# A tap-weighted sum with a routed expert layer: scheduler margins in two phases, constants in a chain of their own, tap weights of two units in the logits' place

## The chip, the cores and the metric

The kernel runs on one core of a Trainium2 chip, whose engines each take their instructions in order and meet through semaphores: PE (matrix products), VectorE (DVE in the profile), ScalarE (ACT), GpSimd (POOL) and SyncE (SP), which issues most of the DMA transfers. The metric is the device time of one execution in microseconds. Before the change three runs took 1194.86, 1198.12 and 1200.12 us, median 1198.12.

## The reference

The input x is 8 sequences of 3584 rows of 192 numbers, in 8 heads of 24. Each row and head has 7 tap weights; their softmax weighs the row and the six before it. The result, 28672 rows, goes through a routed layer of 8 experts, one for each row.

```python
w = softmax(weight_gen, axis=-1)                     # (8, 3584, 8 heads, 7 taps)
x = einsum('bshk,bskhg->bshg', w, windows of 7 rows of x, zeros in front)   # -> (28672, 192)
logits = x @ w_gate                                  # 8 experts
e_idx  = argmax(logits, axis=1)
gate_w = softmax(logits)[row, e_idx]
eom    = sigmoid(x @ w_output_gate)[row, e_idx]
for e in range(8):                                   # rows of expert e only
    out[rows] = gate_w * eom * (relu(x[rows] @ w1[e]) @ w2[e])    # 192 -> 1024 -> 192
```

## The kernel before

The rows are cut into 32 units of 896 (128 partitions by 7 rows). A unit goes through these steps. Its tap weights are loaded (w) and made into a softmax on VectorE and ScalarE. Its seven products of taps and rows are shared: GpSimd makes the first ones (gap), VectorE the others (vap, or vt from unit 7 on). TAPS says how many; 4 of 7 go to GpSimd in units 0 to 6, and 4 to 6 later, by POOL and SHARES. In units 0 to 6 (PE_U) PE adds the seven products up in PSUM with an identity matrix (constants cf); from unit 7 on VectorE adds them. ScalarE and VectorE then split the sum into a high and a low half of 16 bits in a record (rt, three buffers in turn), beginning with the row numbers (rt from tok). That first write needs the scatters of the unit three before, which read the same buffer, to have landed. The record is transposed (gt), by PE and a copy of ScalarE in units below TR_U, by seven DMA transposes on SP's queue in the others. Three matmuls a row group give the logits (gm, gt). VectorE finds the expert (lz to the scan p), PE the ranks (p with upper and ones), and after that the rows' places are known (pos, posi). GpSimd then issues seven indirect transfers that scatter the unit's records into the expert-sorted array srtd in DRAM. p_4 means the scan of unit 4, and so on.

Beside this the weights of the 8 experts are loaded, scaled, split into halves and stored in DRAM (wd). The low halves wa and wpb are VectorE instructions with two inputs in SBUF.

As soon as all weights are there and the first three units have been sorted, tiles of 256, later 384 and 512 rows of one expert are taken from srtd: 77 tiles in all, 229 groups of 128 rows. SP loads a tile's row numbers (meta), its transposed rows (xT) and the expert's two weight arrays (wa, wb). GEMM1 (xT, wa) fills a PSUM bank; ScalarE makes the high half of its relu (hh) and VectorE the low half (hl); GEMM2 (wb with hh and hl) gives the output, which ScalarE scales (ys). The first tiles' output (DEFER of them) goes to DRAM by SP (yd) and is scattered at the end; that of later tiles is scattered by GpSimd at once. Units and tiles run beside each other until the last unit is sorted, near 913 us; then only tiles are left.

The order of every engine's instructions is written when the program is built. Each step above is a chain, a generator that names the engine of its next instruction. A planner keeps a clock and times for each engine; at each step it takes the chain that could go on first by its own estimates, that is by `max(now, c.t - c.slack, c.engine.t - c.engine.lead) - c.favour`, and by rank where these are equal. The numbers behind it are margins: LAT and its kin are added after an instruction until its result counts as there, LEAD is how far SP may be filled ahead, WBX delays the return of a weight buffer, FAVOUR is a table by chain number. They act through the order alone. On the chip every engine goes through its list, and an instruction waits for what it reads.

The PSUM has fixed places: two sums of units (0 and 2560), the tap weights of units below 7 (3904 and 1344), the logits (2048), the turned records (1536), small tables. At the end of the front they become banks of GEMM1 and GEMM2.

Of the kernel before, what the change touches and what calls it, by code (L numbers as in the profile page):

```python
# [67 lines left out]
class Chain:  # L68


    def __init__(self, gen, rank, t, engine):
        self.gen, self.rank, self.t, self.engine, self.gate = gen, rank, t, engine, None
        self.favour = 0.0
        self.slack = EAGER[1] if len(rank) > 1 and rank[0] in EAGER[2] and rank[1] < EAGER[0] else SLACK


class Order:
# [5 lines left out]

    def add(self, gen, rank, engine, t=None):
        c = Chain(gen, rank, self.cur.t if t is None else t, engine)
        c.favour = FAVOUR.get(self.made, 0.0)
# [24 lines left out]
class Queue:  # L111


    def __init__(self, order, engine, cost, issue, lead, host=None):
        self.order, self.engine, self.cost, self.issue, self.lead, self.host = order, engine, cost, issue, 0.0 if host else lead, host
        self.moved = self.issued = 0.0

# [24 lines left out]
class Paced:  # L142


    def __init__(self, order, engine, cost, before=0.0, after=None, lead=0.0, follows=True, holds=None):
        self.order, self.engine, self.cost, self.t = order, engine, cost, 0.0
        self.before, self.after = before, LAT if after is None else after
        self.lead, self.follows, self.holds = lead, follows, holds

    def __getattr__(self, name):  # L150
        f = getattr(self.engine, name)

        def call(*args, **kwargs):
            c, own = self.order.cur, self.cost(name, args, kwargs)
            r = f(*args, **kwargs)  # L155
            if own is not None:
                held = LOCK and self.holds is not None and self.holds(kwargs)
                self.t = max(self.t, (c.t if self.follows else self.order.now) + self.before, self.order.port if held else 0.0) + own
                if held:
                    self.order.port = self.t  # L160
                c.t = max(c.t, self.t + self.after)
            return r

        return call


def two_in_sbuf(kwargs):
    return sum(k in kwargs and kwargs[k].space != bass.MemoryType.PSUM for k in ("in0", "in1", "data0", "data1")) > 1
# [23 lines left out]
def gpsimd_cost(name, args, kwargs):  # L192
    if name == "indirect_dma_start":
        return 0.987
    if name == "memset":
        return 1.0
    return 0.172 + largest(args, kwargs) * 0.002
# [23 lines left out]
def kernel(ctx: ExitStack, tc: tile.TileContext, x, wg, wgate, wogate, w1, w2, cst, out):  # L221
    nc = tc.nc
    od = Order()
    V = Paced(od, nc.vector, vector_cost, holds=two_in_sbuf)
    S = Paced(od, nc.scalar, scalar_cost, after=LAT_S)
    G = Paced(od, nc.gpsimd, gpsimd_cost, holds=lambda kwargs: True)
    T_ = Paced(od, nc.tensor, tensor_cost, after=0.0)
    SP = Queue(od, nc.sync, sync_cost, sync_issue, LEAD)
    TQ = SP if TURN_SP else Queue(od, nc.scalar, sync_cost, sync_issue, LEAD, S)
# [139 lines left out]
    nc.vector.tensor_copy(f_e8, cf[:, o : o + 8])  # L369
# [11 lines left out]
    nc.vector.tensor_copy(f_rr, rr[:, :, 0])  # L381
# [27 lines left out]


# [44 lines left out]
    def weight_steps(stg):  # L455

        for e in range(NE):
            yield from take(st_free, SP)

            st1 = stg.tile([P, 1536], F32, tag="st1", name=f"st1_{e}")  # L460
            st2 = stg.tile([P, 1536], F32, tag="st2", name=f"st2_{e}")
            SP.dma_start(out=st1[:, 0:1024], in_=w1[e, 0:128, :])
            for h in range(2):
                SP.dma_start(out=st1[64 * h : 64 * h + 64, 1024:1536], in_=w1[e, 128:192, 512 * h : 512 * h + 512])
            SP.dma_start(out=st2.rearrange("p (c d) -> p c d", d=D), in_=w2[e].rearrange("(c p) d -> p c d", p=P))
            od.add(split_steps(e, st1, st2), (RANK_W, e), S)
# [3 lines left out]
            od.cur.t = od.now  # L470

    def split_steps(e, st1, st2):
# [18 lines left out]
        for lo, n in ((0, 1024), (2048, 512)):  # L491
            src = st1[:, lo // 2 : lo // 2 + n]
            hi = wah[:, lo : lo + n]
            yield S
            S.activation(hi, src, AF.Copy, scale=s1)
            yield V
            V.scalar_tensor_tensor(out=wah[:, lo + n : lo + 2 * n], in0=src, scalar=s1, in1=hi, op0=ALU.mult, op1=ALU.subtract)
# [15 lines left out]
        S.activation(hi, st2, AF.Copy, scale=s2)  # L513
        yield V
        V.scalar_tensor_tensor(out=wbh[:, 1536:3072], in0=st2, scalar=s2, in1=hi, op0=ALU.mult, op1=ALU.subtract)
# [102 lines left out]
    def acc_steps(u, taps):  # L618
# [8 lines left out]
        while own or left:  # L627
            yield V, lambda: own or gp
            if own and not (n and gp and gp[0][2] <= od.now + SLACK):
# [27 lines left out]
    def used(u, tag):  # L657
# [3 lines left out]
        if tag == "va":  # L661
            (tw_free if u >= PE_U - 2 and d["tw_at"] == 3904 else d["tw_home"]).append((od.cur.t, d["tw_at"]))
# [5 lines left out]
    def add_steps(u, t, tag, kind):  # L668
# [12 lines left out]
        tap_free[tag].append((od.cur.t + LAT_P, kind))  # L681
        if n == K - 1 - PAIRS:
            d["total"] = d["sum"][:, 0 : NV * GD].rearrange("p (a b) -> p a b", b=GD)
            od.add(sum_steps(u), (RANK_B, u), S, T_.t + LAT_P)

    def sum_steps(u):
# [39 lines left out]
        else:  # L726
            od.cur.t += LAT_T
# [36 lines left out]
        od.cur.t += LAT_R  # L764
# [261 lines left out]
    def gemm1_unit(hp, d, u, at):  # L1026
# [10 lines left out]
        od.add(evac_steps(d, ps[:, at : at + nf * T], hh[:, 0 : nf * T], hl[:, 0 : nf * T], at, u), (RANK_H,), S, T_.t + LAT_P)  # L1037
# [10 lines left out]
    def gemm2_group(d, g, at):  # L1048
# [126 lines left out]
    od.add(softmax_steps(0), (RANK_A, 0, 0), V, U[0]["wt"])  # L1175
    od.add(gate_steps(), (RANK_GATE, -1), SP)
# [68 lines left out]
def TAPS(u):  # L1245

    n = PRO_G if u < PE_U else FIRST_G[u - PE_U] if u < PE_U + len(FIRST_G) else SHARES.get(u, POOL[u % len(POOL)])
# [7 lines left out]
LAT = 0.226  # L1255
LAT_S = 0.191
LAT_P = 0.485
LAT_T = 3.005
LOCK = False
LAT_R = 1.0  # L1260
SLACK = 0.026
EAGER = 0, 0.2, (2, 3, 4)
LEAD = 3.739
# [4 lines left out]
AHEAD = 1  # L1268
DELAY = {128: 4, 256: 1, 384: 1, 512: 1}
LATE = 4  # L1270
# [5 lines left out]
PRO_G = 4  # L1276
POOL = (5,5,4)
SHARES = {7: 5, 8: 6, 15: 4, 22: 5, 29: 4, 30: 5}
FAVOUR = {32: 2.7, 117: 2.9, 447: 0.5, 448: 0.4, 553: 1.5, 689: 3.2, 706: 1.8, 874: -0.2, 886: 2.1, 925: 4.0, 941: -0.4, 1008: -1.4}
PE_U = 7  # L1280
GIVE = 1
RANK_X = 2.5
X_EARLY = 3
RANK_GATE = 3.985
FIRST_G = ()
DEFER = 4
WBX = 5.532
# [3 lines left out]
TR_U = 5  # L1291
# [21 lines left out]
```

## Time and profile before

| | before |
|---|---|
| runs, us | 1194.86, 1198.12, 1200.12 (median 1198.12) |
| profiled execution, us | 1196.09 (span 1194.3) |
| PE busy | 1114.0 us, 93% of the span |
| VectorE busy | 944.6 us, 79% |
| ScalarE busy | 594.9 us, 50% |
| GpSimd busy | 857.5 us, 72% |
| granted clock of PE, mean | 0.979 |

The shares are means over a front, where only units are worked on, a middle, where units and tiles run together, and a tail with tiles alone. The busy tenths by slice of a fortieth of the span (29.9 us) show them: PE stands at 6 to 8 in the first eight slices and at 9 after; VectorE at 6 to 8 in the first seven, 9 in the middle and 1 to 3 in the tail. PEclk is the granted clock of PE in tenths of full speed.

### The profile page before, as it was taken

To read this page: it belongs to the slowest core of one execution; us is meant where nothing else is said; L and a number is where in the kernel's file an instruction comes from. 1 tells how busy PE (TensorE), PEld (TensorE's weight loads), DVE (VectorE), ACT (ScalarE), POOL (GpSimd) and SP (SyncE) were. 2 spreads that over 40 slices of the span, in tenths; PEclk is the share of its full clock that TensorE was granted. 3 is DMA by queue.
4 is the path that set the end of the run, shared out by engine and by line. 5 is a ranking of instruction groups with operands and counts; after the bars stand their busy time and mean duration, and the time that the engine had idled before them with its cause. 6 is when DMAs were issued, how large, how long until landed. Compare 5 with 4: busy or idle time off the path is not lost.

```text
span 1194.3 us, 27270 instructions
## 1 busy us (share of the span) xinstructions
PE 1114.0 (93%) x9689; PEld 812.9 (68%) x9689; DVE 944.6 (79%) x2009; ACT 594.9 (50%) x1257; POOL 857.5 (72%) x758
## 2 busy tenths in 40 slices
PE   6978776699999999999999999999999999999897
PEld 2444345577766767777777777777777777899697
DVE  6788966889999999999999999998999763333231
ACT  2857534455555555555555555555555543434342
POOL 5685779777888888888888888888888752422222
PEclk9988898899999999999999999999999999999999
DMA  9896768999998788898688996986877579889992
GB/s 286 262 300 197 235 185 209 261 296 251 247 269 228 226 249 239 238 262 236 190 247 246 252 247 195 270 238 188 256 211 220 163 212 328 254 265 349 328 307 84
DMA packets 274937, 290.40 MB, mean 243 GB/s; under 512 B 213238, under 2 KB 238311, under 8 KB 265072
## 3 DMA queue, kind: packets, MB, share of 16 engines
q1 hardware_dynamic: 252912, 244.06, 70.8%
q0 software_dynamic: 21744, 44.30, 11.8%
q8 instruction: 76, 1.25, 0.4%
q14 instruction: 61, 0.50, 0.1%
q10 hardware_dynamic: 144, 0.29, 0.1%
HBM read 186.54 MB, written 61.42 MB: 208 GB/s over the span
## 4 chain that ended last, share of the span: by engine, by line
PE 65%; DVE 13%; DMA 7%; issue 5%; POOL 4%; SPq 4%; ACT 1%; POOLq 0%; DVEq 0%; ACTq 0%
PE ps L155 65%; DVE ps L155 5%; SPq L129 4%; DVE hl L155 3%; DMA wa<-wd 3%; POOL gap L155 2%; POOL srtd L155 2%; DMA srtd<-rt,posi 1%; DVE vt L155 1%; DMA wd<-wa 1%; DVE rt L155 1%; POOL out_dram L155 1%; DVE wa L155 1%; DVE vap L155 1%; DVE wpb L155 1%
## 5 line engine op out<-in xcount | busy, mean ns | idle before, releaser
L155 PE MATMUL ps<-xT,wa 128*128 128x512 f16 (+3 forms) x2480 | 488.1, 346 | 34.6 <-DVE hl L155 15.8
L155 PE MATMUL ps<-wb,hh 128*128 128x192 f16 x3664 | 472.9, 246 | 0.2 <-DVE hl L155 0.2
L155 PE MATMUL ps<-wb,hl 128*128 128x192 f16 x1832 | 451.1, 246 | 0.0
L155 DVE SCALAR_TENSOR_TENSOR hl<-ps,hh 128x512 f16<-128x512 f32 (+1 forms) x472 | 308.0, 665 | 153.4 <-ACT hh L155 149.4
L155 ACT ACTIVATE hh<-ps 128x512 f16<-128x512 f32 (+1 forms) x472 | 272.8, 583 | 230.7 <-PE ps L155 224.3
L155 PEld LDWEIGHTS <-wa 128*128 128x128 f16 x2480 | 226.7, 98 | 212.6 <-issue 21.3
L155 PEld LDWEIGHTS <-hh 128*128 128x128 f16 x3664 | 333.4, 98 | 43.1 <-issue 1.3
L155 POOL TENSOR_TENSOR gap<-x,w 128x768 f32<-128x768 f32 (+5 forms) x254 | 343.3, 1376 | 23.6 <-PE ps L155 14.2
L155 POOL DMA_INDIRECT out_dram<-ys,meta x221 | 219.4, 993 | 189.7 <-ACT ys L155 143.9
L155 POOL DMA_INDIRECT srtd<-rt,posi x224 | 226.5, 1011 | 85.4 <-issue 56.8
L155 ACT ACTIVATE ys<-ps,sc 128x192 f32<-128x192 f32 x229 | 96.2, 420 | 221.9 <-PE ps L155 157.2
L155 DVE TENSOR_TENSOR ps<-ps,gap 128x1344 f32<-128x1344 f32 x118 | 182.9, 1550 | 3.7 <-POOL gap L155 3.2
L155 PEld LDWEIGHTS <-hl 128*128 128x128 f16 x1832 | 179.6, 98 | 0.1
L155 PE MATMUL ps<-vap,cf 128*128 128x512 f32 (+1 forms) x126 | 60.6, 626 | 16.0 <-DVE vap L155 16.0
L155 POOL TENSOR_TENSOR gap<-halo,w 128x1152 f32<-128x1152 f32 (+5 forms) x38 | 60.0, 1580 | 18.9 <-ACT gt L155 10.8
L155 PE MATMUL ps<-gap,cf 128*128 128x512 f32 x168 | 69.7, 551 | 0.0
L155 DVE SCALAR_TENSOR_TENSOR rt<-ps,sx,rt 128x448 f16<-128x448 f32 x64 | 58.0, 909 | 7.7 <-ACT rt L155 3.8
L155 PE MATMUL ps<-xT,late 128*128 128x128 f16 (+2 forms) x560 | 55.4, 256 | 4.0 <-DMA late<-wd 4.0
L155 PEld LDWEIGHTS ps<-vap,cf 128*128 128x128 f32 x126 | 25.9, 217 | 43.2 <-issue 23.6
L155 PEld LDWEIGHTS ps<-gap,cf 128*128 128x128 f32 x168 | 30.4, 192 | 29.4 <-issue 24.8
L155 DVE TENSOR_TENSOR ps<-ps,vt 128x1344 f32<-128x1344 f32 x32 | 49.7, 1552 | 0.0
L155 DVE TENSOR_TENSOR vt<-x,ps 128x1344 f32<-128x1344 f32 (+2 forms) x39 | 49.6, 1284 | 0.1
(122 smaller groups left out, 813.2 us busy)
## 6 DMA issues: line engine op xcount, KB each, us to landing
wa<-wd SPq DMA_DIRECT2D x62, 1024.0 KB
wb<-wd SPq DMA_DIRECT2D x76, 768.5 KB
x<-in_x_dram SPq DMA_DIRECT2D x32, 672.0 KB
late<-wd SPq DMA_DIRECT2D x14, 1024.0 KB
w<-in_wg_dram SPq DMA_DIRECT2D x32, 196.0 KB
wd<-wpb SPq DMA_DIRECT2D x8, 768.5 KB
st<-in_w_dram SPq DMA_DIRECT2D x8, 768.0 KB
st<-in_w_dram SPq DMA_DIRECT2D x8, 512.0 KB
```

The source lines that it names most:

```text
L129: r = f(*args, **kwargs)
L155: r = f(*args, **kwargs)
```

## The change

The numbers of the planner become two sets, FIRST until its clock is at 395 us and LATER from then on, and many get other values. With LOCK the planner now counts VectorE instructions with two inputs in SBUF and GpSimd's products as excluding each other. A negative favour delays a chain. The constants f_e8 and f_rr are copied in a chain of their own. VectorE's tap weights of units 1 and 2 stand in the logits' place. Units 5 and 6 are turned by PE (TR_U 7). GpSimd's taps fall in units 8 (6 to 4), 12, 27 and 30 (5 to 4) and rise in unit 15 (4 to 5). FRONT, WEIGHT_RANKS and LOW_G change nothing by themselves, since their values are those that held before or are empty.

```diff
 class Order:
+    def m(self, name):
+        return (FIRST if self.now < TURN else LATER)[name]
 ...
-            at = max(self.now, c.t - c.slack, c.engine.t - c.engine.lead)
-            key = (at - c.favour, c.rank)
+            at = max(self.now, c.t - c.slack - min(0.0, c.favour), c.engine.t - c.engine.lead)
+            key = (at - max(0.0, c.favour), c.rank)
 ...
-    nc.vector.tensor_copy(f_e8, cf[:, o : o + 8])
+    e8 = cf[:, o : o + 8]
 ...
-    nc.vector.tensor_copy(f_rr, rr[:, :, 0])
 ...
+    def const_steps():
+        V.tensor_copy(f_e8, e8)
+        V.tensor_copy(f_rr, rr[:, :, 0])
 ...
-        home = tw_free if u >= PE_U else rest_free
+        home = tw_free if u >= PE_U else lg_free if u in TW_LG else rest_free
 ...
+        if u == PE_U - 1:
+            tw_free.extend(f for f in rest_free if f[1] == 3904)
+            rest_free[:] = [f for f in rest_free if f[1] != 3904]
 ...
-        t, _ = sum_free.pop()
-        acc_free.append(t)
+        got = next(f for f in sum_free if f[1] == 2560)
+        sum_free.remove(got)
+        acc_free.append(got[0])
 ...
+    od.add(const_steps(), (RANK_A, 0, 1), V, CONST_AT)
 ...
-LAT = 0.226
 ...
-LEAD = 3.739
+FIRST = {'LAT': 0.083, 'LAT_S': 0.191, 'LAT_P': 0.295, 'LAT_T': 1.952, 'LAT_R': 1.0, 'LOCK': True, 'SLACK': 0.02, 'LEAD': 5.44, 'G_D': 0.987, 'WBX': 3.688}
 ...
+CONST_AT = 10.0
+TW_LG = (1, 2)
-AHEAD = 1
+AHEAD = 2
-LATE = 4
+LATE = 2
-SHARES = {7: 5, 8: 6, 15: 4, 22: 5, 29: 4, 30: 5}
+SHARES = {12: 4, 27: 4, 30: 4}
-GIVE = 1
+GIVE = 2
-DEFER = 4
+DEFER = 6
-TR_U = 5
+TR_U = 7
```

What this does to the order is shown at three places. In the names the first number is that of the unit or tile: gap6_2 is the product of unit 6 and tap 2, p3_4 the scan of unit 4, xT0 the first tile, rt_2_101 the third record buffer (units 2, 5, 8), rt_0_99 the first (units 0, 3, 6).

PE, at the first GEMM1. Before, it stands behind the ranks of unit 4 and one product of unit 6:

```order
L155 MATMUL ps_82<-gap6_1_1305,cf_91 128x512 x2
L155 MATMUL ps_82<-gap6_1_1305,cf_91 128x320
L155 LDWEIGHTS upper_94
L155 MATMUL ps_82<-p3_4_1369,upper_94 128x8
L155 LDWEIGHTS ones16_97
L155 MATMUL ps_82<-p3_4_1369,ones16_97 128x8
L155 MATMUL ps_82<-gap6_2_1364,cf_91 128x512 x2
L155 MATMUL ps_82<-gap6_2_1364,cf_91 128x320
L155 LDWEIGHTS wa2_138
L155 MATMUL ps_82<-xT0_1389,wa2_138 128x256
```

After, it stands behind the last logits of unit 5 and that unit's ranks:

```order
L161 LDWEIGHTS gt5_1420
L161 MATMUL ps_82<-gm_251,gt5_1420 128x32
L161 LDWEIGHTS gt5_1420
L161 MATMUL ps_82<-gm_251,gt5_1420 128x32
L161 LDWEIGHTS upper_94
L161 MATMUL ps_82<-p3_5_1601,upper_94 128x8
L161 LDWEIGHTS ones16_97
L161 MATMUL ps_82<-p3_5_1601,ones16_97 128x8
L161 LDWEIGHTS wa2_136
L161 MATMUL ps_82<-xT0_1306,wa2_136 128x256
```

All 49 products of units 0 to 6 and the turning of unit 5 have moved ahead of it; that of unit 6 now stands between the blocks of the first tile's GEMM1.

SP, between the second and the third tile's loads. Before, the seven transposes of unit 5 stand there (those of unit 6 follow the third tile, those of unit 7 the fifth):

```order
L129 DMA wb1_1485<-wd_79 128x1537
L129 DMA_TRANSPOSE gt5_1518<-rt_2_101 128x3x128 x7
L129 TENSOR_LOAD ti2_0_1058
L129 ISA x2
L1014 ISA
L129 DMA meta2_1603<-srtd_78 128x2x2
L129 ISA
L129 DMA_TRANSPOSE xT2_1605<-srtd_78 128x3x256
L129 ISA
L129 DMA wa1_137<-wd_79 128x2048
L129 ISA
L129 DMA wb2_1608<-wd_79 128x1537
```

After, the third tile (meta2, xT2, wa1, wb2) follows directly on the second, and the loads of units 8 and 9 behind it:

```order
L136 DMA wb1_1364<-wd_79 128x1537
L136 TENSOR_LOAD ti2_0_1056
L136 ISA x2
L1036 ISA
L136 DMA meta2_1436<-srtd_78 128x2x2
L136 ISA
L136 DMA_TRANSPOSE xT2_1438<-srtd_78 128x3x256
L136 ISA
L136 DMA wa1_135<-wd_79 128x2048
L136 ISA
L136 DMA wb2_1441<-wd_79 128x1537
L136 DMA halo_83<-in_x_dram 112x1152
```

The first DMA transposes are now those of unit 7, and stand behind the sixth tile's load.

ScalarE, at the record of unit 6, which waits for the landing of unit 3. Before, it stands between two high halves (hh0) of the first tile:

```order
L155 ACTIVATE rt_1_100<-ez4_1424,isx4_1134 128x7
L155 ACTIVATE hh0_0_1444<-ps_82 128x512
L155 ACTIVATE hh0_1_1529<-ps_82 128x512
L155 ACTIVATE rt_0_99<-tok_102 128x7x2
L155 ACTIVATE rt_0_99,ssq6_1561<-ps_82 128x7x192
L155 ACTIVATE hh0_2_1549<-ps_82 128x512
L155 ACTIVATE rt_0_99<-ps_82,sx6_1568 128x7x192
L155 ACTIVATE hh0_3_1579<-ps_82 128x512
```

After, it stands ahead of the last copy of unit 5's turned rows, and all high halves follow later:

```order
L161 COPY gt5_1420<-ps_82 128x768
L161 CAST posi4_1506<-pos4_1503 128x7
L161 ACTIVATE rt_1_100<-ez4_1465,isx4_1151 128x7
L161 COPY gt5_1420<-ps_82 128x768
L161 ACTIVATE w8_1285<-w8_1285 128x392
L161 ACTIVATE rt_0_99<-tok_102 128x7x2
L161 ACTIVATE rt_0_99,ssq6_1565<-ps_82 128x7x192
L161 COPY gt5_1420<-ps_82 128x384
L161 ACTIVATE rt_0_99<-ps_82,sx6_1577 128x7x192
```

On GpSimd the scatters of units 3 and 4 alternated; after, all seven of unit 3 are issued ahead of unit 4's.

## Rows read from the trace of the kernel before

**Rows 1.** Windows of the whole run: us, each engine's busy time (instructions), PEclk, DMA share, GB/s.

```profile
0.00:163.00 163.00, 129.00 (x510) 66.44 (x511) 130.29 (x274) 91.66 (x151) 109.86 (x90) 0.94 0.79 246
163.00:193.00 30.00, 16.36 (x85) 10.11 (x84) 12.98 (x43) 10.28 (x20) 25.51 (x23) 0.83 0.84 221
193.00:305.00 112.00, 98.40 (x982) 80.94 (x979) 102.17 (x235) 55.97 (x137) 86.55 (x75) 0.95 0.93 260
305.00:500.00 195.00, 189.82 (x1661) 136.98 (x1662) 187.83 (x400) 103.03 (x228) 166.23 (x148) 0.99 0.86 245
500.00:913.00 413.00, 411.55 (x3631) 295.74 (x3629) 397.14 (x819) 220.32 (x479) 361.64 (x320) 1.00 0.82 230
913.00:1195.00 282.00, 268.88 (x2829) 222.67 (x2826) 114.19 (x243) 113.65 (x245) 107.71 (x107) 0.99 0.81 254
```

**Rows 2.** Waits of PE, whole run: us in total, times, longest us.

```profile
PE ps L155 <- DVE hl L155: 16.0, 12, 10.3
...
PE ps L155 <- DMA wa<-wd: 11.9, 7, 5.0
```

**Rows 3.** Timeline of PE: start, duration, instructions [idle before <- releaser].

```profile
187.86 2.29 PE L155 MATMUL ps<-xT,wa 128*128 128x256 f16 x10 [10.31 <-DVE hl L155]
...
192.90 0.33 PE L155 MATMUL ps<-wb,hh 128*128 128x192 f16 x2
...
214.66 1.67 PE L155 MATMUL ps<-xT,wa 128*128 128x256 f16 x7 [6.56 <-DVE ez L155]
...
238.61 1.49 PE L155 MATMUL ps<-xT,wa 128*128 128x384 f16 x5 [4.96 <-DMA wa<-wd]
```

**Rows 4.** Timeline of ACT.

```profile
150.37 0.80 ACT L155 COPY gt<-ps 128x768 f16<-128x768 f16 x1 [2.58 <-PE ps L155]
...
184.97 0.22 ACT L155 ACTIVATE rt<-tok 128x14 int32<-128x14 f32 x1 [9.44 <-DMA srtd<-rt,posi]
```

**Rows 5.** Timeline of SP's queue.

```profile
176.33 10.48 SPq L129 DMA_TRANSPOSE gt<-rt  x7
...
217.60 9.81 SPq L129 DMA_TRANSPOSE gt<-rt  x7
...
231.24 0.42 SPq L129 DMA_DIRECT2D wa<-wd  x1
```

**Rows 6.** Timeline of DVE at the start.

```profile
4.45 0.17 DVE L369 COPY ps<-cf 128x8 f32<-128x8 f32 x1 [4.45 <-DMA cf<-in_cst_dram]
...
6.00 0.57 DVE L155 TENSOR_REDUCE ps<-w 128x56 f32<-128x392 f32 x1
```

**Rows 7.** Timeline of DVE, units 3, 4 and 5.

```profile
157.00 0.20 DVE L155 TENSOR_REDUCE pos<-pe 128x7 f32<-128x56 f32 x1
...
163.14 0.26 DVE L155 TENSOR_TENSOR_SCAN p<-segs,ps 128x56 f16<-128x56 f16 x1
...
205.49 0.26 DVE L155 TENSOR_TENSOR_SCAN p<-segs,ps 128x56 f16<-128x56 f16 x1
```

**Rows 8.** Timeline of POOL.

```profile
99.70 2.22 POOL L155 TENSOR_TENSOR gap<-halo,w 128x1152 f32<-128x1152 f32 x1 [10.75 <-ACT gt L155]
...
158.87 0.98 POOL L155 DMA_INDIRECT srtd<-rt,posi  x1 [2.25 <-ACT rt L155]
...
163.78 2.72 POOL L155 TENSOR_TENSOR gap<-x,w 128x576 f32<-128x576 f32 x2
...
178.12 0.98 POOL L155 DMA_INDIRECT srtd<-rt,posi  x1 [0.30 <-issue]
```

**Rows 9.** Groups of PE by form, 0 to 170 us: busy us, mean ns.

```profile
L155 PE MATMUL ps<-ident,rt 128*128 128x128 f16 x105 | 10.2, 236 | 1.4 <-DVE ps L155 1.4
```

**Rows 10.** Groups of DVE by form, whole run.

```profile
L155 DVE TENSOR_TENSOR vt<-x,ps 128x1344 f32<-128x1344 f32 x24 | 37.0, 1541 | 0.0
```

**Rows 11.** Timeline of DVE, low halves of two experts' weights.

```profile
106.91 3.46 DVE L155 SCALAR_TENSOR_TENSOR wa<-st,wsc,wa 128x512 f16<-128x512 f32 x1
...
125.42 0.69 DVE L155 SCALAR_TENSOR_TENSOR wa<-st,wsc,wa 128x512 f16<-128x512 f32 x1
```

More of the change, by code (lines that the diff above doesn't have):

```diff
@@ L73, in __init__ @@
         self.favour = 0.0
-        self.slack = EAGER[1] if len(rank) > 1 and rank[0] in EAGER[2] and rank[1] < EAGER[0] else SLACK
+        self.slack = 0.0
 class Order:
@@ L111, with __init__, lead @@
 class Queue:
-    def __init__(self, order, engine, cost, issue, lead, host=None):
-        self.order, self.engine, self.cost, self.issue, self.lead, self.host = order, engine, cost, issue, 0.0 if host else lead, host
+    def __init__(self, order, engine, cost, issue, host=None):
+        self.order, self.engine, self.cost, self.issue, self.host = order, engine, cost, issue, host
         self.moved = self.issued = 0.0
+    @property
+    def lead(self):
+        return 0.0 if self.host is not None else self.order.m("LEAD")
     @property
@@ L142, with __init__ @@
 class Paced:
-    def __init__(self, order, engine, cost, before=0.0, after=None, lead=0.0, follows=True, holds=None):
+    def __init__(self, order, engine, cost, after, holds=None):
         self.order, self.engine, self.cost, self.t = order, engine, cost, 0.0
-        self.before, self.after = before, LAT if after is None else after
-        self.lead, self.follows, self.holds = lead, follows, holds
+        self.after, self.lead, self.holds = after, 0.0, holds
     def __getattr__(self, name):
@@ L156, in call, with two_in_sbuf @@
             if own is not None:
-                held = LOCK and self.holds is not None and self.holds(kwargs)
-                self.t = max(self.t, (c.t if self.follows else self.order.now) + self.before, self.order.port if held else 0.0) + own
+                held = self.order.m("LOCK") and self.holds is not None and self.holds(name, kwargs)
+                self.t = max(self.t, c.t, self.order.port if held else 0.0) + own
                 if held:
                     self.order.port = self.t
-                c.t = max(c.t, self.t + self.after)
+                c.t = max(c.t, self.t + (self.order.m(self.after) if self.after else 0.0))
             return r
         return call
-def two_in_sbuf(kwargs):
-    return sum(k in kwargs and kwargs[k].space != bass.MemoryType.PSUM for k in ("in0", "in1", "data0", "data1")) > 1
+def two_in_sbuf(name, kwargs):
+    return name in ("tensor_tensor", "scalar_tensor_tensor") and sum(k in kwargs and kwargs[k].space != bass.MemoryType.PSUM for k in ("in0", "in1", "data0", "data1")) > 1
 def largest(args, kwargs):
@@ L189, in scalar_cost, with gpsimd_cost @@
     return own + (0.2 if "accum_out" in kwargs else 0.0) + (0.0 if isinstance(kwargs.get("scale", 1.0), float) else 0.1)
[L192 removed]
+def gpsimd_cost(name, args, kwargs, scatter):
     if name == "indirect_dma_start":
[L194 removed]
+        return scatter
     if name == "memset":
         return 1.0
[L197 removed]
+    return 0.13 + largest(args, kwargs) * 0.00184
 def tensor_cost(name, args, kwargs):
@@ L223 @@
     od = Order()
[L224 to L229, printed above, removed]
+    V = Paced(od, nc.vector, vector_cost, "LAT", holds=two_in_sbuf)
+    S = Paced(od, nc.scalar, scalar_cost, "LAT_S")
+    G = Paced(od, nc.gpsimd, lambda *o: gpsimd_cost(*o, od.m("G_D")), "LAT", holds=lambda name, kwargs: name in ("tensor_tensor", "scalar_tensor_tensor"))
+    T_ = Paced(od, nc.tensor, tensor_cost, None)
+    SP = Queue(od, nc.sync, sync_cost, sync_issue)
+    TQ = SP if TURN_SP else Queue(od, nc.scalar, sync_cost, sync_issue, S)
     B, SEQ, D = x.shape
@@ L470, in weight_steps, with halves @@
             od.cur.t = od.now
+    def halves(which, hi, low, src, scale):
+        if which in LOW_G:
+            S.activation(src, src, AF.Copy, scale=scale)
+            S.copy(hi, src)
+            yield G
+            G.tensor_tensor(out=low, in0=src, in1=hi, op=ALU.subtract)
+        else:
+            S.activation(hi, src, AF.Copy, scale=scale)
+            yield V
+            V.scalar_tensor_tensor(out=low, in0=src, scalar=scale, in1=hi, op0=ALU.mult, op1=ALU.subtract)
     def split_steps(e, st1, st2):
@@ L489, in split_steps @@
         wah = wa.bitcast(F16)
-        for lo, n in ((0, 1024), (2048, 512)):
+        for part, (lo, n) in enumerate(((0, 1024), (2048, 512))):
             src = st1[:, lo // 2 : lo // 2 + n]
@@ L494, in split_steps @@
             yield S
-            S.activation(hi, src, AF.Copy, scale=s1)
-            yield V
-            V.scalar_tensor_tensor(out=wah[:, lo + n : lo + 2 * n], in0=src, scalar=s1, in1=hi, op0=ALU.mult, op1=ALU.subtract)
+            yield from halves((e, part), hi, wah[:, lo + n : lo + 2 * n], src, s1)
         yield SP
@@ L512, in split_steps @@
         S.activation(wb.bitcast(F32)[:, 1536:1537], inv[:, 0:1], AF.Copy, scale=inv[:, 1:2])
-        S.activation(hi, st2, AF.Copy, scale=s2)
-        yield V
-        V.scalar_tensor_tensor(out=wbh[:, 1536:3072], in0=st2, scalar=s2, in1=hi, op0=ALU.mult, op1=ALU.subtract)
+        yield from halves((e, 2), hi, wbh[:, 1536:3072], st2, s2)
         st_free.append(od.cur.t)
@@ L628, in acc_steps @@
             yield V, lambda: own or gp
-            if own and not (n and gp and gp[0][2] <= od.now + SLACK):
+            if own and not (n and gp and gp[0][2] <= od.now + od.m("SLACK")):
                 k = own.pop(0)
```

42 lines of the change are left out of this document (21 added, 21 removed).

## The prediction

> **What bounds the kernel now.** I read the windows first, cut where the kernel changes its nature [rows 1]. Until 163 us no engine is the bound: PE and VectorE are each busy about 130 us, so the end of this stretch is set by the chain from unit to unit. From 163 to 193 the first tile starts and everything starves: PE 16.4 of 30 us, VectorE 13.0, granted clock 0.83. From 193 to 305 (the first nine tiles) PE works 98.4 of 112 us. From 305 to 913 it works 601.4 of 608 and VectorE 585.0, so both are nearly full. In the last 282 us PE has 268.9 and VectorE only 114. What can be won lies before 305; what can be lost lies between 305 and 913, where VectorE has 23 us left over.
>
> The waits of PE name the pieces [rows 2], and its timeline gives the dates [rows 3]. At 187.86 PE resumes after 10.31 us without work, and that block of ten matmuls took 2.29 us, which I put down to the lower clock around it. At 214.66 it has waited 6.56 us in the unit chain, at 238.61 4.96 us for a tile's weights. The first GEMM2 is at 192.90. The causes stand on other engines. ScalarE's record write of unit 6 (rt from tok) sat from 175.5 to 184.97 on the landing of unit 3's scatters, and the next hh of the first tile is behind it [rows 4]. SP's queue spent 10.48 us and later 9.81 us on seven transposes each between tile loads; after the second group a tile's weights were asked for only at 231.24, and PE's 4.96 us followed [rows 5].
>
> **The change part by part.** Sums are against the profiled execution, 1196.1 us, 2 us under the median of the runs (1198.1). The work that an order puts before a given instruction I took by giving each instruction its group's mean duration in the trace of before, less the 0.06 us by which neighbours overlap where stretches are compared.
>
> *Constants.* VectorE waited 4.45 us for cf, then did memsets and two copies until 6.00, when the first softmax began without a wait [rows 6]. After, the memsets run while cf and w are on their way, and the copies (0.17 and 0.19 us) come behind two products. The first softmax can start when w is there, somewhere before 6.00. Bounds 0 and -4.4; I take -1.5, the memsets and copies that stood behind cf, and count it in the date of p_5 below.
>
> *Unit chain and the first tile.* Before, GEMM1 began directly behind p_4's ranks; after, behind p_5's, with all 49 taps and five more turn rounds ahead of it. VectorE's work up to the scan of p_5 falls from 171.8 to 153.2 us; up to p_4's, dated 163.14, it was 143.7 [rows 7]. With the same idle time p_5's scan comes at 163.1 + 153.2 - 143.7 = 172.6. But it hangs on the landing too: ScalarE now has unit 6's record write ahead of unit 5's last gt copy. In before unit 3's position came at 157.00 and its first scatter at 158.87; its last was issued at 178.12, since POOL alternated units 3 and 4, and landed 6.85 us later [rows 4, 7, 8]. After, VectorE has 9.8 us less ahead of that position, which gives about 146; seven scatters at 0.98 with a little between them and four products of 2.72 follow in one run [rows 8], so the last is issued near 166 and has landed at 173. Record write, squares, copy and logits take some 4 us, the rank chain 3.5: p_5's scan at 177 to 181 (before: 205.49). VectorE then has 9.3 us ahead of the first tile's first low half, while PE does GEMM1 and turns unit 6. First GEMM2 near 189: -4.
>
> The two added transposed units cost PE 42 transposes at 10.2/105 = 0.097 us [rows 9], 4.1 us, and ScalarE eight copies of at most 0.80 [rows 4]. They lie mostly beside the chain before 189; at worst the full 4.1 adds. TAPS of units 1 and 2 in the logits' place only delay unit 0's logits, at 60 us or so, covered by products; bounds 0 and +6.6, the one wait of PE in the unit chain that the rows price [rows 3]; taken 0.
>
> *First nine tiles.* The three tile loads stand together in SP's queue, and fourteen of its transposes, 20.3 us [rows 5], are gone; so the 6.56 and the 4.96 us should go [rows 3]. The order puts 95.2 us of PE work between the first and the tenth tile (before 96.0) and 93.2 of VectorE's (before 102.8), so PE decides. Before needed 112 with 13.6 of it idle; I expect about 4 idle, -9 to -10, since some waits return: three banks instead of four until unit 6 is turned, and unit 7's seven transposes come just behind tile 6's load. Tenth tile near 291 instead of 305: -14. Bounds -22 (every idle microsecond from 163 to 305 except the chain's) and 0.
>
> *Tiles ten to 45.* SHARES moves four products from GpSimd to VectorE, 4 x 1.54 = 6.2 us [rows 10], and work that the front no longer does comes here as well: VectorE's order holds 604.7 us in this stretch, before 592.0, against 598.5 of PE in both. Before took 608 us. VectorE would fill 99% of that, so some low halves come late; I take +4. Bounds: 0, if the idle share of PE hides it, and +13, if VectorE keeps the ratio of before (592.0/608, so 604.7 takes 621). GpSimd had 80 us free there [rows 1], so nothing is gained by its relief.
>
> *Tail.* Same order of SP and PE to a few places, VectorE at 40%: 0. Two more tiles' outputs (DEFER) go through DRAM and back, one issue each way on a queue that then has room.
>
> Sum: 1196.1 - 14 + 4 = 1186; the profile lies 2 us under the median, and I put half of that on: **1187 us**.
>
> [...] A 128x512 low half took 3.46 us at 106.91 beside GpSimd's products and 0.69 us at 125.42 beside none [rows 11]: 2.8 us per such meeting. [...]
>
> **The rivals.** *(a) The landing still gates the front.* For: ScalarE's write of unit 6 still needs unit 3's landing, and now p_5, the first tile and everything behind it wait for it, where before two hh were already done. Against: seven scatters run ahead of unit 4's. If POOL keeps 4.6 us instead of 12 us (its work before that scatter fell only from 120.8 to 116.2), the last is issued at 173.5, p_5 is at 186 and GEMM2 at 199: +6 there, -9 in the nine tiles, +4: 1197, no change. Its 10.75 us idle at 99.70 [rows 8] is what could free it earlier.
>
> *(b) VectorE becomes the bound from the first tile to the 45th.* This ends slower. Between the first low half and tile 46 the new order has 697.9 us of VectorE work; before 694.8 in some 725 us, a share of 0.958. At that share it takes 728, from 188 to 916: 1199, and the front gained nothing because PE runs out of low halves. Below 0.95 it decides the sign: at 0.945 it is 738 us, 926 in place of 913, 1209. For: 99% in the middle. Against: PE set the pace before, and VectorE's idle time was waiting for it.
>
> *(c) Everything idle before 305 goes.* If p_5 comes at 173 as VectorE's work alone says and no wait returns, tile ten starts at 283, 22 earlier, and the middle costs 1: 1175. For: three tiles ahead. Against: SP still carries unit transposes from unit 7 on.
>
> *(d) The change does nothing that the time shows*: the same 77 tiles and GEMMs, waits only moved. That is the sum of (a), priced with it.
>
> **How the numbers follow.** Forecast (1181 to 1193) 0.42; (a) and (d), 1193 to 1200, 0.22; (b), mean 1207, 0.16; (c), 1168 to 1181, 0.20. A difference under 0.5% (1192.1 to 1204.1) cannot be told from no change here. Faster: 0.38 of the forecast, all of (c), 0.02 of (a): 0.60. Same: 0.04, 0.20 of (a) and 0.01 of (b): 0.25. Slower: 0.15. For 8 times in 10 I go from 1172, which leaves out a tail of (c), to 1204, which leaves out most of (b).
>
> **What would show it.** Right, step by step: VectorE's first reduce before 5 us; p_5's scan between 177 and 181 and the first GEMM2 near 189; no idle of over 3 us on PE between 189 and 291; 22 groups of GEMM2 done near 291 (it was 305); from there to the 46th tile some 612 us instead of 608, with VectorE above 0.97. Wrong: unit 3's last scatter after 172 (a); PE waiting for hl by tens of us between 300 and 900 (b); a wait for wa or for unit 7's transposes that takes the place of the two removed.

## The result: 1180.3 us, 1.4% faster

| | before | after |
|---|---|---|
| runs, us (median, lowest to highest) | 1198.0 (1194.86 to 1200.12, 4 runs) | 1180.26 (1179.65 to 1183.15, 4 runs) |
| ratio, 95% interval | | 0.9859 [0.9832, 0.9886] |
| profiled execution, us | 1196.09 (span 1194.3) | 1180.51 (span 1178.8) |
| PE busy, us | 1114.0 | 1113.7 |
| VectorE busy, us | 944.6 | 947.7 |
| GpSimd busy, us | 857.5 | 848.5 |
| mean granted clock of PE | 0.979 | 0.986 |

Executions far above the others of their kernel (the highest, one of six of e12, took 6252.74 us) are left out of the ratios below.

PE's busy time is the same, so nearly all of the 15.5 us between the two spans is idle time of PE: 80.3 us before, 65.1 after. The windows of the kernel after, cut as in [rows 1] but for the end, say where. The columns are those of [rows 1]: busy time (and count) of PE, its weight loads, VectorE, ScalarE and GpSimd, then PE's granted clock, the DMA share and GB/s.

```profile
0.00:163.00 163.00, 131.28 (x535) 68.34 (x536) 128.44 (x288) 95.46 (x160) 120.88 (x97) 0.94 0.84 269
163.00:193.00 30.00, 24.26 (x221) 19.05 (x219) 24.51 (x65) 15.26 (x33) 24.83 (x22) 0.88 0.70 236
193.00:305.00 112.00, 108.70 (x1057) 88.84 (x1055) 108.15 (x242) 61.39 (x152) 86.35 (x75) 1.00 0.98 272
305.00:500.00 195.00, 190.35 (x1673) 135.90 (x1672) 188.56 (x380) 100.52 (x223) 162.23 (x145) 1.00 0.83 229
500.00:913.00 413.00, 401.54 (x3520) 286.27 (x3519) 397.86 (x832) 214.60 (x473) 357.59 (x316) 1.00 0.82 230
913.00:1180.00 267.00, 257.55 (x2737) 215.27 (x2734) 100.16 (x214) 107.62 (x230) 96.66 (x99) 0.99 0.83 259
```

PE's idle time falls from 13.6 to 5.7 us between 163 and 193 and from 13.6 to 3.3 between 193 and 305, where the granted clock is now 1.00 instead of 0.95. It rises from 1.5 to 11.5 us between 500 and 913. So the change wins in the front, gives a good half of it back in the middle, and wins a little at the end. To date the steps I count GEMM2's groups of 128 rows (8 matmuls of wb and hl each). The counting windows of the kernel after, PE's column with the count in brackets:

```profile
0.00:280.00 280.00, 42.20 (x172) 0.95 0.87 267
280.00:282.00 2.00, 1.09 (x5) 1.00 0.87 240
282.00:900.00 618.00, 275.50 (x1120) 1.00 0.83 233
900.00:904.00 4.00, 1.97 (x8) 1.00 1.20 265
904.00:1179.00 275.00, 129.89 (x528) 0.99 0.82 254
```

The first nine tiles are 22 groups, 176 matmuls. Here the 176th ends at 281.10 us, before at 303.12. At 903.13 us 1304 matmuls are done (one that lies across an edge counts in two windows) and 528 are left; the kernel before stood there at 912.54. The three stretches are these, each to the end of its last such matmul:

| stretch | before, us | after, us | difference | forecast |
|---|---|---|---|---|
| start to the tenth tile | 303.1 | 281.1 | -22.0 | -14 |
| tenth to 46th tile | 609.4 | 622.0 | +12.6 | +4 |
| 46th tile to the end | 281.8 | 275.7 | -6.1 | 0 |

The windows of the middle stretch, before and after, and PE's waits for hl in them (us, times, longest):

```profile
303.12:912.54 609.42, 602.54 (x5297) 433.31 (x5296) 586.27 (x1223) 324.07 (x708) 529.44 (x467) 1.00 0.83 235
PE ps L155 <- DVE hl L155: 2.7, 5, 0.8
281.10:903.13 622.03, 605.55 (x5318) 433.48 (x5318) 598.83 (x1260) 324.08 (x716) 532.21 (x471) 1.00 0.83 233
PE ps L161 <- DVE hl L161: 12.3, 22, 1.2
```

VectorE has 12.6 us more to do there and the stretch is 12.6 us longer; PE's waits for hl are 9.6 us more of it.

The front. The timeline of PE in the kernel after, as in [rows 3] (start, duration, engine, line, operation, tiles, shape and, in brackets, the idle time before it and what ended it):

```profile
172.94 0.17 PE L161 MATMUL ps<-p,upper 128*128 128x8 f16 x1 [2.04 <-DVE p L161]
...
174.84 4.42 PE L161 MATMUL ps<-xT,wa 128*128 128x256 f16 x20 [1.70 <-DMA x<-in_x_dram]
...
185.78 0.33 PE L161 MATMUL ps<-wb,hh 128*128 128x192 f16 x2
```

ScalarE's there, as in [rows 4]:

```profile
168.61 0.22 ACT L161 ACTIVATE rt<-tok 128x14 int32<-128x14 f32 x1 [1.13 <-issue]
```

GpSimd's, as in [rows 8]:

```profile
143.10 0.98 POOL L161 DMA_INDIRECT srtd<-rt,posi  x1 [2.54 <-ACT rt L161]
...
161.33 0.98 POOL L161 DMA_INDIRECT srtd<-rt,posi  x1 [0.30 <-issue]
```

And SP's queue, as in [rows 5]:

```profile
145.41 0.41 SPq L136 DMA_DIRECT2D meta<-srtd  x1
...
149.58 0.40 SPq L136 DMA_DIRECT2D meta<-srtd  x1
...
157.52 0.38 SPq L136 DMA_DIRECT2D meta<-srtd  x1
```

Unit 3's scatters ran from 143.10 to 161.33 (before 158.87 to 178.12), so ScalarE's record write of unit 6 began at 168.61 without waiting for a landing; before it sat 9.44 us [rows 4]. p_5's ranks stand at 172.94, the first GEMM1 at 174.84, the first GEMM2 at 185.78 (192.90 in [rows 3]). The first three tiles' loads began at 145.41, 149.58 and 157.52 on SP; before, the third tile's came behind the first seven transposes of [rows 5]. In PE's waits the entries of [rows 2] changed places:

```profile
PE ps L161 <- DVE hl L161: 15.6, 28, 1.2
...
PE ps L161 <- DMA late<-wd: 0.2, 1, 0.2
```

No wait for a tile's weights (11.9 us before) is left but 0.2 us in the tail. The waits for hl add up to the same, but they are 28 of at most 1.2 us, most of them in the middle, where before one of 10.3 us in the front made up most of the sum. At the start, VectorE's first reduce stands at 4.79 instead of 6.00 [rows 6], what it waits for now is w, and the copies of the constant cf, which stood at 4.45, come behind it, the first here at 12.23. VectorE's timeline:

```profile
4.79 0.57 DVE L161 TENSOR_REDUCE ps<-w 128x56 f32<-128x392 f32 x1 [2.85 <-DMA w<-in_wg_dram]
...
12.23 0.39 DVE L161 COPY ps<-cf 128x8 f32<-128x8 f32 x2
```

### The profile page after: what moved, and what is told of

The parts are those of the page before. It is cut to its first block, busy times and chain, and to the rows that moved or that the text cites. A ratio compares the mean times of both kernels' runs of the same rounds, so it can differ in the third digit from the quotient of the medians.

```text
span 1178.8 us, 27377 instructions
## 1 busy us (share of the span) xinstructions
PE 1113.7 (94%) x9731; PEld 813.7 (69%) x9731; DVE 947.7 (80%) x2017; ACT 594.8 (50%) x1267; POOL 848.5 (72%) x750
## 3 DMA queue, kind: packets, MB, share of 16 engines
q0 software_dynamic: 21744, 44.30, 12.6%
## 4 chain that ended last, share of the span: by engine, by line
PE 31%; DVE 22%; POOL 5%; issue 5%; DMA 3%; ACT 1%; DVEq 0%; POOLq 0%; SPq 0%; ACTq 0%
PE ps L161 31%; DVE ps L161 11%; DVE hl L161 5%; POOL gap L161 3%; DVE vt L161 2%; DVE rt L161 1%; POOL srtd L161 1%; POOL out_dram L161 1%; DMA x<-in_x_dram 1%; ACT rt L161 1%; DMA wb<-wd 1%; DMA out_dram<-ys,meta 1%; DMA late<-wd 0%; DVE w L161 0%; ACT hh L161 0%
## 5 line engine op out<-in xcount | busy, mean ns | idle before, releaser
L161 PE MATMUL ps<-xT,wa 128*128 128x512 f16 (+3 forms) x2440 | 483.6, 346 | 12.6 <-DVE hl L161 10.0
L161 POOL DMA_INDIRECT out_dram<-ys,meta x216 | 214.2, 992 | 194.4 <-ACT ys L161 135.0
L161 POOL TENSOR_TENSOR gap<-x,w 128x576 f32<-128x576 f32 (+5 forms) x249 | 333.3, 1363 | 23.9 <-issue 11.6
L161 POOL DMA_INDIRECT srtd<-rt,posi x224 | 229.1, 1023 | 90.4 <-issue 58.0
L161 DVE TENSOR_TENSOR ps<-ps,gap 128x1344 f32<-128x1344 f32 x114 | 177.2, 1554 | 5.1 <-POOL gap L161 4.7
L161 PE MATMUL ps<-vap,cf 128*128 128x512 f32 (+1 forms) x126 | 55.9, 587 | 13.0 <-DVE vap L161 13.0
L161 POOL TENSOR_TENSOR gap<-halo,w 128x1152 f32<-128x1152 f32 (+4 forms) x35 | 58.6, 1673 | 9.5 <-DVE w L161 5.1
L161 DVE TENSOR_TENSOR ps<-ps,vt 128x1344 f32<-128x1344 f32 x36 | 55.9, 1553 | 0.0
L161 DVE TENSOR_TENSOR vt<-x,ps 128x1344 f32<-128x1344 f32 (+2 forms) x44 | 55.5, 1275 | 0.2
L161 ACT ACTIVATE rt<-ps 128x1344 bf16<-128x1344 f32 x32 | 41.3, 1290 | 19.2 <-DVE ps L161 11.6
```

## The experiments

Each kernel ran beside the kernel before on the same chip: e1 to e4 on one chip, e5 to e8 on a second, e9 to e12 on a third. On the first two the kernel before took 5.8 and 5.9% longer than in the first comparison (1267.4 and 1268.7 us), for a reason that e5 shows in part; on the third it took 1197.9 us. So ratios are compared on one chip, or between chips on which the kernel before took the same.

**e4: the landing alone.** Kernel before, order unchanged, unit 6's record in a buffer of its own.

```diff
+        if u == 6:
+            ri = rt6
         d["ri"], rt = ri, ri.bitcast(F16)
```

> The kernel before with a record buffer of its own for unit 6, so that the write of rt from tok no longer waits for the landing of unit 3's scatters; order of every engine the same. Theory: the 9.44 us wait of ScalarE and the 10.31 us of PE at 187.86 go, the first GEMM2 comes 7 to 9 us earlier, and at least half of it reaches the end (4 to 8 us faster than before), about half of what the change won in the front. Rival: the transposes on SP's queue and the unit chain (6.56 and 4.96 us on PE) grow by as much: 0 to 2 us faster.

Ratio 0.9993 [0.9958, 1.0027]. ScalarE no longer waits, and the first GEMM2 comes at 186.45 us (191.64 in e2), but PE then waits for the weights of the next tiles. The timeline of ScalarE in e4:

```profile
174.10 0.21 ACT L155 ACTIVATE rt<-tok 128x14 int32<-128x14 f32 x1
```

Of SP's queue:

```profile
176.57 10.30 SPq L129 DMA_TRANSPOSE gt<-rt  x7
...
190.33 0.42 SPq L129 DMA_DIRECT2D wa<-wd  x1
...
192.62 11.42 SPq L129 DMA_TRANSPOSE gt<-rt  x7
...
207.69 0.42 SPq L129 DMA_DIRECT2D wa<-wd  x1
```

And of PE:

```profile
196.27 2.36 PE L155 MATMUL ps<-xT,wa 128*128 128x256 f16 x20 [1.60 <-DMA wa<-wd]
...
213.65 2.31 PE L155 MATMUL ps<-xT,wa 128*128 128x256 f16 x10 [8.84 <-DMA wa<-wd]
...
237.51 1.78 PE L155 MATMUL ps<-xT,wa 128*128 128x384 f16 x5 [3.93 <-DMA wa<-wd]
```

The third tile's wa is asked for at 190.33, behind seven transposes, the fourth's at 207.69, behind seven more; PE waits 1.60, 8.84 and 3.93 us. By 305 us 168 matmuls with hl are done, as many as in e2, the kernel before on the same chip with four products made twice. The rival holds as far as the front shows: the stall of 10.31 us was real, and taking it away alone won nothing in the first nine tiles, because the weights were late behind it. The interval of the whole time leaves room for 5 us of gain, so it does not decide by itself.

**e5: the kernel after, unchanged, and e7: the transposes alone.** e7 puts the fourteen transposes of units 5 and 6 back on SP's queue, the rest of the order held.

```diff
         d["split"] = True
+        if u in (5, 6):
+            for j in range(JS):
+                nc.sync.dma_start_transpose(out=spare[:, j], in_=rt[:, j, 0:384])
```

> The kernel after, unchanged, beside the kernel before on the chip of these runs. Theory: the change is worth the 1.2 to 1.7% that the first comparison gave. Rival: the doubled products and the constants of the first four runs lay on a chip where every kernel took 6% longer, and on such a chip the change is worth nothing or costs up to 1%.

> The kernel after with the fourteen DMA transposes of units 5 and 6 back on SP's queue (seven behind the second tile's load, seven behind the loads of units 8 and 9 and ahead of the fourth tile's), their result left unused; all other orders unchanged. Theory: SP's queue in the front is what the change freed; the third and fourth tile's weights come late again, PE waits 4 to 9 us for wa between 190 and 250 us and the end is 3 to 8 us later. Rival: the three tiles loaded ahead cover it: under 1.5 us.

e5: 1276.3 against 1268.7 us, ratio 1.0064 [1.0034, 1.0093]. e7: 1278.2 us, 1.0072 [1.0043, 1.0101]. On that chip the change costs 0.6%, and the transposes add 1.9 us that the intervals do not separate from nothing. In e7's queue the third tile's load moves to 164.84 and the fourth's to 188.80, and no wait for wa appears. The first GEMM1 there is at 174.08, so three tiles are asked for ahead of it and the transposes are covered; that they are gone is not what freed the front, as far as that chip shows it. e4 has the early landing without the tiles loaded ahead, and it is not enough; the tiles ahead without the early landing were not tried, so that it takes both is likely and not shown.

What differs on that chip shows in PE's rows. The waits of PE in e5 over the whole run (us in total, times, longest):

```profile
PE ps L161 <- issue: 42.0, 62, 3.9
```

A stretch of e5's PE timeline in the middle:

```profile
466.97 0.21 PE L161 MATMUL ps<-gm,gt 128*128 128x32 f16 x2 [0.54 <-issue]
467.69 0.18 PE L161 MATMUL ps<-gm,gt 128*128 128x32 f16 x1 [0.51 <-issue]
468.39 0.21 PE L161 MATMUL ps<-gm,gt 128*128 128x32 f16 x2 [0.53 <-issue]
469.10 0.18 PE L161 MATMUL ps<-gm,gt 128*128 128x32 f16 x1 [0.50 <-issue]
469.82 0.31 PE L161 MATMUL ps<-gm,gt 128*128 128x32 f16 x6 [0.54 <-issue]
```

PE stops 62 times for 42.0 us in all with nothing to wait for that the profile shows, often in trains: here it starts one or two matmuls each 0.7 us. In the first comparison this entry was 0.2 us before and is not in the list after. The pauses come in the kernel before as well (32.4 us in e2). Milestones by the same count, in us (e2 is the kernel before with four products doubled, below, on the chip of e1 to e4; before itself was not profiled on these two chips):

| | first GEMM2 | tenth tile | 46th tile | end |
|---|---|---|---|---|
| before, first comparison | 192.9 | 309.8 | 914.8 | 1194.3 |
| after, first comparison | 185.8 | 285.3 | 905.3 | 1178.8 |
| e2, chip of e1 to e4 | 191.6 | 315.1 | 981.2 | 1268.3 |
| e5, chip of e5 to e8 | 186.1 | 300.8 | 985.7 | 1271.7 |

(Here each date is that of the first such matmul behind the milestone.) The gain in the front falls from 25 to 14 us, the loss in the middle grows from 15 to 19, and the gain at the end falls from 6 to 1. In the middle e2 takes 61 us longer than before in the first comparison and e5 65 longer than after. Pauses are only 21.6 and 28.4 us of that; PE's busy time grows by 19.5 and 26.2 us (from 600.1 to 619.6 and from 603.8 to 630.0), at a granted clock of 0.98 and 0.97 for 1.00; the rest are other waits. In the front after loses 15 us and before, which had idle time there, 5. So part of why the sign turned can be placed, but what makes PE pause on these chips stays open.

**e1, e2, e6: more work on VectorE.** Four products of the middle are made twice, orders unchanged.

```diff
+                if eng is V and u in (8, 12, 27, 30) and k == 6:
+                    nc.vector.tensor_tensor(...)        # the same product once more
```

> The kernel after, with VectorE's product of tap 6 in units 8, 12, 27 and 30 made twice into the same place (four times 1.54 us, 6.2 us of VectorE work more in the middle; every engine's order otherwise the same). Theory: VectorE sets the pace between about 300 and 910 us, so most of it reaches the end: 4 to 6 us slower than the kernel after, PE's waits for hl up by as much. Rival: PE sets the pace there and its 11.5 us of idle time between 500 and 913 came from single meetings: 0 to 1.5 us slower.

> The kernel before with the same four products doubled, order otherwise the same. Theory: in the kernel before PE set the pace from 305 to 913 (601 of 608 us busy) and VectorE had some room, so the cost is smaller than in the kernel after: 0 to 3 us. Rival: VectorE at 96% was as full as it gets there too: 5 to 6 us slower.

> Run again beside the kernel after on one chip: VectorE's product of tap 6 in units 8, 12, 27 and 30 made twice, orders unchanged, 6.2 us more VectorE work. Theory: VectorE sets the pace in the middle: 3 to 6 us slower than the kernel after. Rival: PE sets it: 0 to 1.5 us.

e1: 1.0122 [1.008, 1.0165], on a chip without a run of after as it is. e6: 1.0083 [1.0051, 1.0115], 3.9 us over e5 on the same chip; e2: 1.001 [0.9984, 1.0036], 1.2 us over before. The 6.2 us of work cost some 4 us in after and 1 in before, as the theory says, but the intervals overlap and the pauses lie over it: suggestive, no more.

**e8 and e9: the shares of before, e10: still fewer products on VectorE.**

```diff
-SHARES = {12: 4, 27: 4, 30: 4}
+SHARES = {7: 5, 8: 6, 15: 4, 22: 5, 29: 4, 30: 5}   # e8, e9
+SHARES = {8: 6, 14: 5, 20: 5, 26: 5}                # e10
```

> The kernel after with the shares of before (GpSimd 6 taps in unit 8, 5 in units 12, 27, 30, 4 in unit 15): four products off VectorE, the front up to the third tile unchanged, the planner's order after that different. Theory: VectorE's work was what PE waited for in the middle; PE's idle time from 500 to 913 us falls from 11.5 to 4 to 7 and the end is 3 to 7 us earlier. Rival: GpSimd or the order of the middle holds it up: no gain, or some us slower.

> The kernel after with the shares of before, a second time, as the reference for the next kernel. Theory (VectorE sets the pace in the middle): about 0.4% faster than the kernel after, which stood at 0.9859 of before in the first comparison and at 1.0064 on a chip where every kernel took 6% longer. Rival: no difference, the first reading was the order's luck.

> The kernel after with eight products fewer on VectorE (four fewer than before had): GpSimd makes 6 in unit 8, 5 in units 12, 14, 20, 26, 27, 30. Theory: VectorE's work between the first tile and tile 46 falls by 12 us and PE's waits for it with it: 6 to 12 us faster than the kernel after. Rival: GpSimd, at 87% in the middle, gets 22 us more and becomes what VectorE and the scatters wait for: no faster than with the shares of before, or slower.

e8, on the chip with the pauses: 1270.9 us, 5.4 under e5 (1.001 [0.9983, 1.0037]), just what the theory expected. But its profile has 26.3 us of pauses, e5's 42.0, and its gain does not lie where the products were moved: from the tenth to the 46th tile it takes 692.7 us (e5: 691.3), behind it 279.2 (e5: 288.2). e9, where before takes what it took in the first comparison: 1210.2 us, ratio 1.0109 [1.0085, 1.0132], against 0.9859 for after. e10: 1211.2 us, 1.0121 [1.0099, 1.0143]. So these kernels are 2.5 and 2.7% slower than after, and the gain that the theory expected did not come. The rows say where the time went. VectorE's waits for GpSimd's products from 305 to 913 us in after (us, times, longest):

```profile
DVE ps L161 <- POOL gap L161: 4.4, 4, 1.3
```

The same in e9:

```profile
DVE ps L161 <- POOL gap L161: 9.0, 5, 2.4
```

In e10:

```profile
DVE ps L161 <- POOL gap L161: 15.8, 12, 2.4
```

PE's waits for hl in the same stretch, 12.1 us in after, in e9:

```profile
PE ps L161 <- DVE hl L161: 23.5, 32, 2.4
```

And in e10:

```profile
PE ps L161 <- DVE hl L161: 30.9, 37, 2.5
```

Of the products handed to GpSimd more come later than VectorE wants them: 4.4, 9.0, 15.8 us of waits (1.0 in before). In after one addition had waited 1.17 us for such a product and began at 549.55; the low half next but one behind it began at 551.44, and PE's next block of GEMM1 at 552.17, after 1.22 us that ended on hl. That the other waits pass on to PE in the same way is my reading, no run separates it. Not all of the 30 us is that: PE's waits for hl grow by 11.4 us in e9 and 18.8 in e10; e9's first nine tiles end 6.7 us later, and PE's busy time is 7.9 us longer at a clock of 0.980. The order behind the third tile is another one too.

The stretches of the first table, for all kernels on chips without the pauses, show that GpSimd is at most a part (us; the last three columns are of the middle stretch). e11, whose order is that of after up to the planner's 395 us, reaches the tenth tile within 1.0 us of it, so the two chips can be compared:

| | to the tenth tile | tenth to 46th | 46th to the end | VectorE busy | PE waits for hl | VectorE waits for gap |
|---|---|---|---|---|---|---|
| before | 303.1 | 609.4 | 281.8 | 586.3 | 2.7 | 1.0 |
| after | 281.1 | 622.0 | 275.7 | 598.8 | 12.3 | 4.4 |
| e9 | 287.8 | 642.6 | 275.2 | 603.0 | 23.9 | 9.0 |
| e10 | 281.2 | 651.0 | 274.6 | 603.9 | 31.6 | 15.8 |
| e11 | 280.1 | 630.4 | 275.8 | 601.5 | 15.9 | 3.7 |
| e12 | 306.5 | 642.9 | 274.8 | 610.7 | 19.9 | 0.4 |

e12 (below) has the shares of after, hardly waits for GpSimd, and takes as long in the middle as e9. And e9 and e10 did not take work off VectorE where it was scarce: with four and eight products fewer it had 4.2 and 5.1 us more to do in the middle than in after, because other work of the units came forward from behind the 46th tile (99.1 and 94.9 us of VectorE's work there, 110.0 in after). So e9 and e10 do not test whether VectorE sets the pace in the middle, and what the shares are worth apart from the order is not shown.

**e11: one phase, e12: the tap weights' old place.**

```diff
-TURN = 395
+TURN = 1e9             # e11
-TW_LG = (1, 2)
+TW_LG = ()             # e12
```

> The kernel after with the first phase's margins to the end (TURN beyond the planner's time); everything until its 395 us is the same, and after it the order differs in some hundred places. Theory: the front carries the gain and the second set of margins moves at most 3 us either way. Rival: the late set (rank margin 0.676, turn margin 2.466, weight buffers held 5.724) is what keeps PE fed in the middle: 4 us or more slower.

> The kernel after with the tap weights of units 1 and 2 in their old places (TW_LG empty); the order differs from the first unit on, the first GEMM1 still behind p_5. Theory: the place of two units' weights moves only the first 60 us, and its worth at the first GEMM2 is under 2 us either way. Rival: with two places for the weights VectorE runs ahead less, and the first GEMM2 comes 3 us later or more.

e11: 1189.2 us, 0.9925 [0.991, 0.994]: without the second set this order loses 0.66 of the 1.41 points, nearly all in the middle stretch (630.4 us for 622.0). PE's waits from 305 to 913 in e11:

```profile
PE ps L161 <- DVE hl L161: 15.3, 23, 1.5
PE ps L161 <- DMA wa<-wd: 4.5, 1, 4.5
```

Hl is late for 3.2 us more than in after, and one tile's weights come 4.5 us late. e12: 1227.7 us, 1.0239 [1.0219, 1.026], slower than before by 2.4%. Of the 45.4 us that its span is over after's, 25.4 are lost up to the tenth tile and 20.9 between the tenth and the 46th. The front's rows:

```profile
198.33 2.29 PE L161 MATMUL ps<-xT,wa 128*128 128x256 f16 x10 [9.56 <-DVE rt L161]
...
208.90 0.33 PE L161 MATMUL ps<-wb,hh 128*128 128x192 f16 x2 [0.74 <-DVE hl L161]
```

The first GEMM2 is at 208.90 (185.78 in after), PE having sat 9.56 us on a unit's record. The rivals hold in both. The 20.9 us in the middle lie long behind the first 60 us, where the place of these weights is used: there it is the changed order that costs. In e12 the rest of the numbers stayed those chosen for the new place, so it shows what this order loses without it, not what the place would be worth alone.

**e3: the constants.** Copies back at the head of VectorE's list, all other orders held.

```diff
+    nc.vector.tensor_copy(f_e8, e8)                    # ahead of the memsets, as before
```

> The kernel after with the two constant copies back at the head of VectorE's list, the planner's account and all other orders unchanged. VectorE then waits for cf until 4.45 us and its first reduce comes near 4.7 to 6.0 instead of 4.79. Theory: the chain from unit to unit carries a late start to the first tile and the end: 0.5 to 1.5 us slower. Rival: a later wait swallows it: within 0.3 us.

Ratio 1.009 [1.006, 1.0121], on the chip without a run of after; VectorE's first reduce came at 6.21 us. Its interval holds e5's 1.0064, from another chip: inconclusive.

## Why the prediction was right, step by step

It was right in sign, size and range on the chip of the first comparison (1187 said, 1180.3 measured); on e5's chip the same change cost 0.6%, for which it had no term. Three terms were mis-sized, by -8, +8.6 and -6.1 us. That they nearly offset is luck.

*Unit chain.* I dated p_5's scan at 177 to 181 because of the landing; it came at 172.62, and its ranks at 172.94. The failed number is the run of unit 3's scatters, which I ended near 166: it began at 143.10 and ended at 161.33, so nothing waited for the landing. The 172.6 that I had by VectorE's work alone came out by luck: up to that scan VectorE was busy for 134.4 us, 4.0 more than up to p_4's before, where I had 9.5 more, and idle for 38.2, 5.5 more, where I had the same. The first GEMM2 came at 185.78 for 189.

*First nine tiles.* I had -14 in sum and it is -22.0. The windows from the first GEMM2 to the end of the ninth tile, before and after:

```profile
192.90:303.12 110.22, 96.88 (x975) 80.26 (x972) 100.53 (x227) 54.80 (x134) 84.79 (x74) 0.95 0.93 259
185.78:281.10 95.32, 92.39 (x920) 77.51 (x918) 93.10 (x193) 51.00 (x126) 71.17 (x63) 1.00 0.97 272
```

7.1 us are the first GEMM2's (I had 4), 10.4 are idle time of PE, 13.3 before and 2.9 after (I had 9 to 10), and 4.5 are PE's busy time, which I had not counted in the sum. My count of the order's work gave 0.8 of these 4.5; the rest I put down to the granted clock, 0.95 before and 1.00 after, though no run shows it apart. Of the cause that I gave, the transposes off SP's queue are not it: e7 has them back at no cost that can be told.

*Middle.* I took +4 out of 0 to +13, and it is +12.6. The upper bound had VectorE keep its ratio of before, and it did: busy for 586.3 of 609.4 us before and for 598.8 of 622.0 after, 0.96 both times. I had said that it would fill 99% of the stretch and go above 0.97 in any case; the failed step is that PE's idle time would hide most of VectorE's added work. That work came out as I had counted it (12.6 us for 12.7), and the stretch grew by all of it. I also said that nothing would be gained by GpSimd's relief. VectorE's waits for it (4.4 us in after, 9.0 and 15.8 in e9 and e10) show that its dates cost VectorE time although its share left room; what the relief is worth these runs do not show, since e12 loses as much without such waits.

*Tail.* I had 0; it is -6.1. The wait of 4.0 us for a late weight is 0.2 now, and PE's busy time behind the 46th tile is 267.4 us instead of 269.3. Why the late weights came in time was not tried. The stretch is not one of tiles alone, as I had described it: the last unit's scan stands at 963.63 before and at 940.78 after.

*Meetings of VectorE and GpSimd.* My sum has no term for fewer of them. The 24 low halves of the weights took VectorE 43.2 us for 46.8 before, 3.6 us less, while GpSimd's products up to 163 us nearly kept their means (1.68 us for 1.66 at 768, 1.88 for 1.95 at 960). So VectorE saved something and these means of GpSimd show no cost of it; no run has LOCK alone, so whose doing it is stays open.

*Rivals.* (c), everything idle in the front goes, was the nearest for the front, with (b)'s loss in the middle. (a) was ruled out by GpSimd's dates: unit 3's last scatter at 161.33, not behind 172. What freed the front is narrowed down and not shown: the early landing alone does not do it (e4), SP's queue without the transposes is not needed for it (e7), and LOCK, the favours and the tiles loaded ahead were not tried apart. The start is 1.2 us earlier on VectorE (1.5 said); e3 could not tell what of it reaches the end.

## What to carry to other kernels

A stall that ends last in a profile can have another right behind it: taking away 10.31 us of it won nothing in the front (e4), and the transposes that had made the weights late, put back into the new order, cost nothing that can be told (e7). An engine's share of a stretch does not say when its results come: from 305 to 913 us GpSimd is busy for 519.8 us in after and 518.6 in e9, and VectorE waits for it for 4.4 us in the one and 9.0 in the other. Before an experiment is read, look whether it did what it was meant to: e9 takes four products off VectorE, and in the stretch that mattered VectorE had 4.2 us more to do. And numbers of a planner that were chosen together are worth something together: undoing one of them cost 2.5% (e9), 0.7% (e11) and 3.9% (e12), together five times what the whole change brings, so such an experiment tells what the order needs and not what the part is worth.

## What the runs showed of the hardware

On two of the chips PE stood still for 26 to 45 us in each profiled run (e1 to e8) with no semaphore to wait for that the profile shows, often in trains, the one shown with starts 0.7 us apart (466.97, 467.69, 468.39 in e5). The kernel before took 5.8 and 5.9% longer there, the kernel after 8.1%. On such a chip the change that won 1.4% elsewhere lost 0.6%, and one and the same kernel was 0.4% faster than after (e8) where elsewhere it was 2.5% slower (e9). The page of after lists two DMA queues of kind instruction, q8 with 77 packets and q14 with 62 in the whole run. In the train shown neither moved any: between 464 and 472 us of e5 only two queues moved packets (packets, MB, share of the 16 DMA engines):

```profile
q0 software_dynamic: 287, 0.56, 19.4%
q1 hardware_dynamic: 532, 0.02, 4.1%
```

What PE does wait for in the pauses stays open.
